# Attention and two feed-forward layers on one core: head pairs of one token block last, first quads in another product order, second token pair's down pass in halves, weight steps reordered

## The chip, the cores and the metric

The kernel runs on one core of a Trainium2 chip. The metric is the device time of one execution in microseconds. The engines are named as the profile names them: PE (TensorE matmuls), PEld (its weight loads), DVE (VectorE), ACT (ScalarE), POOL (GpSimd) and SP (SyncE, here the queue that issues nearly all DMAs; SPq in the trace).

## The reference

```python
# q, k, v: (4, 12, 448, 64); w_in (768, 2048), moe_w_out (2048, 768)
# w_gate, w_val (768, 1536), moe2_w_out (1536, 768); the weights arrive as float64
q_n, k_n = rmsnorm(q, g_q), rmsnorm(k, g_k)
attn = softmax(q_n @ k_n^T / 8)
x = (attn @ v).transpose(0, 2, 1, 3).reshape(1792, 768)
h = np.maximum(x @ w_in, 0.0)
x = h * h @ w_out                               # layer 0
g = x @ w_gate
out = (g * sigmoid(g) * (x @ w_val)) @ w_out2   # layer 1
```

## The kernel before, in words

The 1792 tokens are four token blocks of 448, one for each batch; channels and hidden units lie on the 128 partitions. All arrays between the stages live in one tile, `xacc`, cut into 24 slots of 128x448; slot 6t+c holds channel block c of token block t.

**Attention** runs over 24 head pairs (`pairs`, six for each token block, in the order of the blocks). For each pair the loop issues score matmuls, exponentials, sums and the product with v. The last step of a pair is long: sums are copied out of PSUM, sent to another layout by DMA, added (`total`, L648, POOL), inverted (`recip`, L654, DVE), sent through DRAM and broadcast (`rb<-row`), and only then multiplied in (`xnorm`, L665, POOL); it comes two to three pairs later, and for the last pairs inside the first layer, through a list `drain`.

**Up passes.** x @ w_in (layer 0) and x @ w_gate, x @ w_val (layer 1) are done by a Strassen-Winograd form: for a pair of token blocks (`tp` 0 or 1) and a "quad" of two weight columns blocks (`q_`), seven products P1 to P7 of sums of weight quarters and sums of input quarters. The input operands are B11, B21, B22 and T1 to T4, where T1 to T4 are differences made by `combine` (L124, 128x1344, DVE) in place of the quarter they replace. Each operand is split into a high part (`hi3`, L141, ACT) and a low part (`lo3`, L145, DVE or POOL) in one of 14 "units" (tiles xab, xat, xbb, xbt, xlast). The table `where` says which unit holds which operand. A product (`group`, L881) is 9 matmuls: three channel blocks by high-high, high-low, low-high. PSUM accumulates over products: chain c1 is P1 then P2, c2 is P5 then P3, c3 is P6 then P7 then P4, and `after` (L846 and L849) reads a chain out after each product, so the next product of a chain waits for that read-out. One call of `step` is one product, with the read-out and what the schedule adds to it.

The order of all work on each engine is written out by hand. `plan_types` lists at which step each operand is made. The weight operands come from a generator, `stream`: `convert` turns a float64 slab that a DMA brought (L213) into float32 by four instructions (ACT L243, DVE L244, DVE L224 twice), `block` splits a weight operand into one of five `ring` buffers (ACT L367, DVE L227). `pump(budget)` is called in every step and issues the next stream instructions until the DVE budget is spent or an instruction's gate is closed. The first two quads are interleaved (`paired`), the others follow one by one (`mid`).

**Down passes.** The hidden arrays are written to DRAM (`send`, L842). At the end of an up pass, the stream goes on with the down weights, half rows of 128x384, whose high and low parts go to units that the last quad has freed (`wunits`, gated by `state["down"]`). In the down pass an "item" is 18 matmuls (L1058, 3.65 us of them): for tokens blocks 0 and 1 together it is one hidden block times three output blocks (first half of the outputs, then second half), for blocks 2 and 3, one after the other, one hidden block times six output blocks. `stage` (L998) reads hidden arrays back, four items ahead; `cleave` splits them two items ahead (ACT L1010, DVE L846 at 128x448) into the units `hunits`; the finished outputs are copied out by L1078 and L1080.

## Time and profile before

| | |
|---|---|
| median of 3 runs | 1260.59 us (1260.13 to 1262.28) |
| the profiled execution's own time | 1261.24 us |
| its span | 1259.1 us |
| PE busy | 1194.9 us (95%), 6416 matmuls |
| DVE, ACT, POOL busy | 810.5, 592.0, 376.1 us |
| attention | start to 253.2 us |
| layer 0, up and down | 253.2 to about 743 us |
| layer 1, up and down | about 743 to 1259 us |

Busy is the time in which an engine executed something; a PE that is busy can still run at half its clock, which the column PEclk shows (1.00 is 2.4 GHz, 0.50 is 1.2 GHz). Matmuls are counted in a stretch with those that overlap its borders.

### The profile page before, as it was taken

To read this page: it belongs to the slowest core of one execution; us is meant where nothing else is said; L and a number is where in the kernel's file an instruction comes from. 1 tells how busy PE (TensorE), PEld (TensorE's weight loads), DVE (VectorE), ACT (ScalarE), POOL (GpSimd) and SP (SyncE) were. 2 spreads that over 40 slices of the span, in tenths; PEclk is the share of its full clock that TensorE was granted. 3 is DMA by queue.
4 is the path that set the end of the run, shared out by engine and by line. 5 is a ranking of instruction groups with operands and counts; after the bars stand their busy time and mean duration, and the time that the engine had idled before them with its cause. 6 is when DMAs were issued, how large, how long until landed. Compare 5 with 4: busy or idle time off the path is not lost.

```text
span 1259.1 us, 17643 instructions
## 1 busy us (share of the span) xinstructions
PE 1194.9 (95%) x6416; PEld 1003.0 (80%) x6416; DVE 810.5 (64%) x1177; ACT 592.0 (47%) x1029; POOL 376.1 (30%) x314
## 2 busy tenths in 40 slices
PE   8999999887999995989999999999999996989998
PEld 5556555476999994868999999999999995879997
DVE  7778988776867756776622439767766768773221
ACT  6877886544666545454421344434334343442121
POOL 6889999455001100000010444222312312000000
PEclk9999999998999997999999999999999998999999
DMA  5344341111643436665522202322432326662331
GB/s 157 97 130 122 95 117 46 27 57 34 208 149 116 142 121 218 203 209 181 172 68 66 59 8 98 105 94 66 133 97 89 102 70 210 202 228 83 115 103 59
DMA packets 109190, 146.64 MB, mean 116 GB/s; under 512 B 13104, under 2 KB 101936, under 8 KB 109104
## 3 DMA queue, kind: packets, MB, share of 16 engines
q1 hardware_dynamic: 108784, 145.52, 37.3%
q8 instruction: 50, 0.82, 0.3%
q14 instruction: 36, 0.29, 0.1%
q10 hardware_dynamic: 320, 0.00, 0.0%
HBM read 114.03 MB, written 31.28 MB: 115 GB/s over the span
## 4 chain that ended last, share of the span: by engine, by line
PE 42%; DVE 4%; ACT 2%; issue 1%; DMA 1%; POOL 0%; SPq 0%; ACTq 0%; DVEq 0%
PE ps L881 23%; PE ps L1058 20%; DVE conv L224 2%; DMA xacc<-hid 1%; DVE conv L244 1%; ACT conv L243 0%; POOL xab L145 0%; DVE xab L846 0%; DVE xacc L846 0%; ACT xab L1010 0%; DVE xbt L846 0%; ACT xacc L849 0%; DVE xbt L227 0%; SPq L998 0%; DVE xacc L124 0%
## 5 line engine op out<-in xcount | busy, mean ns | idle before, releaser
L846 POOL TENSOR_TENSOR xacc<-xacc 128x448 f32<-128x448 f32 x76 | 101.1, 1338 | 357.2 <-ACT xacc L849 260.4
L881 PE MATMUL ps<-xat,ring 128*128 128x448 f32 x720 | 160.5, 374 | 15.4 <-DVE xacc L846 8.1
L881 PEld LDWEIGHTS ps<-xat,ring 128*128 128x128 f32 x720 | 139.0, 194 | 27.9 <-issue 8.4
L224 DVE SCALAR_TENSOR_TENSOR conv<-xacc,conv 128x384 int32<-128x384 int32 (+1 forms) x184 | 149.5, 813 | 4.4
L846 DVE TENSOR_TENSOR xacc<-ps,xacc 128x448 f32<-128x448 f32 x188 | 115.4, 619 | 54.4 <-PE ps L881 52.7
L881 PE MATMUL ps<-xbt,ring 128*128 128x448 f32 x540 | 119.8, 370 | 8.7 <-ACT xbt L141 4.6
L227 DVE TENSOR_TENSOR ring<-conv,ring 128x384 fp32r<-128x384 f32 x120 | 83.7, 699 | 65.4 <-ACT ring L367 63.8
L881 PE MATMUL ps<-xbb,ring 128*128 128x448 f32 x540 | 118.5, 369 | 3.0 <-ACT xacc L849 3.0
L881 PE MATMUL ps<-xab,ring 128*128 128x448 f32 x540 | 117.0, 366 | 1.9 <-ACT xacc L849 1.9
L881 PEld LDWEIGHTS ps<-xbt,ring 128*128 128x128 f32 x540 | 102.4, 190 | 18.2 <-ACT xbt L141 5.0
L881 PEld LDWEIGHTS ps<-xbb,ring 128*128 128x128 f32 x540 | 102.6, 190 | 11.7 <-ACT xacc L849 3.4
L881 PEld LDWEIGHTS ps<-xab,ring 128*128 128x128 f32 x540 | 101.3, 188 | 11.1 <-ACT xacc L849 2.3
L367 ACT CAST ring<-conv 128x384 fp32r<-128x384 f32 x120 | 60.9, 510 | 100.9 <-PE ps L881 59.3
L568 DVE TENSOR_REDUCE mxz<-s 112x2 f32<-112x896 f32 x96 | 99.7, 1086 | 11.9 <-PE s L565 11.6
L846 DVE TENSOR_TENSOR xat<-xacc,xat 128x448 fp32r<-128x448 f32 x65 | 44.7, 701 | 93.2 <-ACT xat L1010 93.2
L600 POOL TENSOR_TENSOR sg<-p 112x896 f32<-112x896 f32 x46 | 98.9, 2151 | 16.3 <-ACT p L596 16.3
L849 ACT ACTIVATE xacc<-xacc 128x448 f32<-128x448 f32 x132 | 75.8, 577 | 53.9 <-DVE xacc L846 52.3
L596 ACT ACTIVATE p<-s 112x896 f32<-112x896 f32 x96 | 87.9, 920 | 22.2 <-PE s L594 16.7
L849 ACT ACTIVATE xacc<-ps 128x448 f32<-128x448 f32 x108 | 58.2, 543 | 75.9 <-PE ps L881 66.4
L1010 ACT CAST xat<-xacc 128x448 fp32r<-128x448 f32 x65 | 35.6, 563 | 95.7 <-PE ps L1058 70.4
L846 DVE TENSOR_TENSOR xab<-xacc,xab 128x448 fp32r<-128x448 f32 x48 | 29.3, 623 | 78.6 <-ACT xab L1010 74.3
L244 DVE TENSOR_SCALAR conv<-conv 128x384 int32<-128x384 int32 (+1 forms) x96 | 51.6, 537 | 43.5 <-ACT conv L243 41.5
(128 smaller groups left out, 2121.8 us busy)
## 6 DMA issues: line engine op xcount, KB each, us to landing
xacc<-hid SPq DMA_DIRECT2D x168, 224.0 KB
hid<-xacc SPq DMA_DIRECT2D x112, 224.0 KB
xacc<-in_moe_w_out_dram SPq DMA_DIRECT2D x56, 384.0 KB
xacc<-in_moe_w_in_dram SPq DMA_DIRECT2D x12, 768.0 KB
xacc<-in_moe_w_gate_dram SPq DMA_DIRECT2D x12, 768.0 KB
xacc<-in_moe_w_val_dram SPq DMA_DIRECT2D x12, 768.0 KB
raw<-in_k_dram SPq DMA_DIRECT2D x24, 224.0 KB
raw<-in_q_dram SPq DMA_DIRECT2D x24, 224.0 KB
```

The source lines that it names most:

```text
L224: nc.vector.scalar_tensor_tensor(out=out, in0=in0, scalar=scalar, in1=out, op0=op, op1=ALU.bitwise_or)
L227: nc.vector.tensor_tensor(out=out, in0=a, in1=b, op=ALU.subtract)
L244: yield dve(0.6 * cost, lambda: nc.vector.tensor_scalar(out=ci, in0=ci, scalar1=3, scalar2=0x7FFFFFFF, op0=ALU.logical_shift_left, op1=ALU ...
L367: fn(*args)
L568: nc.vector.tensor_reduce(out=mxz[:, c, 0:P:D], in_=ps[:CP, :, :S], op=ALU.max, axis=AX.X)
L596: nc.scalar.activation(out=p, in_=ps[:CP, :, :S], func=AF.Exp)
L600: nc.gpsimd.tensor_tensor(out=sg, in0=p_t[pi, 2 * w], in1=p_t[pi, 2 * w + 1], op=ALU.add)
L846: eng.tensor_tensor(out=o, in0=a, in1=b, op=op)
L849: nc.scalar.activation(out=slot(s), in_=src, func=func)
L881: nc.tensor.matmul(ps, w[:, wi, kk * P:(kk + 1) * P], xk[:, xi, kk * S:(kk + 1) * S], start=bool(first and mm == 0), stop=(mm == 3 * KT - ...
L1010: nc.scalar.copy(k[:, 0], src)
L1058: nc.tensor.matmul(ps[t, o], w[:, wi, o % KT * P:(o % KT + 1) * P], h[:, hi], start=(f == 0 and n == 0), stop=(f == nf - 1 and n == 2),)
```

## The change

What it does, by parts:

- **Attention.** The last three head pairs of token block 2 are done after those of block 3. The four `combine`s of token pair 0 stand at pairs 15, 17, 19 and 20 (before: 19 to 22); T1 and T3 of token pair 0 are split in the last two iterations. `prep_early` issues two stream instructions for DVE in pairs 3 to 8, then one, and none from pair 21 on (before: one from pair 3 to the end). The first four weight slabs land in `xacc` slots 16 to 23, two buffers, and the single buffer `wraw` is gone.
- **First quads.** The products go P1, P5, P3, P6, P7, P2, P4 (before P1, P2, P5, P6, P3, P7, P4), each for both quads and one token pair, then for both quads and the other. P3 is now copied out by ACT and added to P1 on POOL, P6 is added to that by DVE. The eight PSUM banks are fixed tiles handed out first in, first out. The `drain` and the operand plans are rewritten for the new order.
- **Down pass, layer 0.** Token blocks 2 and 3 are done as a pair, in halves of the outputs, as blocks 0 and 1 are; the operands of layer 1's up pass are made earlier, their low parts on DVE and no longer on POOL. `cleave` is split in a high and a low part, the read-out of a finished half stands ahead of them, and `stage` behind.
- **Down weights.** The stream's order within and between half rows is changed so that the next half's ACT instruction is issued between two DVE instructions of this one. The pump's budget in the last quad is 1.2 a step (before 1.6), in a down item 1.0 and 1.05 (before 2.1).

The diff, cut:

```diff
-    hunits = ((3, 10), (2, 12))
-    wunits = ((0, 7, 4, 11, 1, 8, 2, 9, 5, 12, 6), (13, 5, 7, 6, 10, 11, 0, 1))
+    hunits = ((3, 10), (4, 9))
+    wunits = ((0, 7, 4, 11, 1, 8, 2, 9, 5, 12, 6), (13, 2, 1, 12, 0, 3, 7, 5))
...
-    loose = set()
+    loose = set(range(16, 24))
...
-                at_ = ("nat",) if ph == 0 and n < 2 else (0, 1) if n < 2 or f == 0 else (2, 3)
+                at_ = (0, 1) if (ph and n < 2) or f == 0 else (2, 3)
...
-        paired = [(p, q_) for p in ("P1", "P2", "P5", "P6", "P3", "P7", "P4") for q_ in range(2)]
+        paired = [(p, q_) for p in ("P1", "P5", "P3", "P6", "P7", "P2", "P4") for q_ in range(2)]
...
-            late = None
-            for n in range(2 * NF[ph]):
+            late, n_w = None, 2 * NF[ph]
+
+            def half_ops(n):
+                nonlocal i
                 c = convs[i % NCONV][:, :KH]
+                i += 1
+                return c, convert(i - 1, c, 0.5)
+
+            cur = half_ops(0)
+            yield next(cur[1])
+            for n in range(n_w):
+                c, ops = cur
...
+                ops = list_ops = [op for op in (next(ops, None), next(ops, None)) if op]
+                rest = cur[1]
+                if ops:
+                    yield ops[0]
+                if n + 1 < n_w:
+                    cur = half_ops(n + 1)
+                    yield next(cur[1])
+                if ops:
+                    yield ops[1]
                 if late:
                     yield late
-                yield act(nc.scalar.copy, t[:, 0], c)
+                yield from rest
+                yield act(nc.scalar.copy, t[:, 0], c, gate=lambda n=n, ph=ph: state["down"] >= 100 * ph + n // 6)
                 late = dve(0.55, low_half, ph, n, t, c)
...
-            pairs = [(b, hp) for b in range(B) for hp in range(NPAIR)]
+            pairs = [(b, hp) for b in range(2) for hp in range(NPAIR)] + [(2, hp) for hp in range(KT)]
+            pairs += [(3, hp) for hp in range(NPAIR)] + [(2, hp) for hp in range(KT, NPAIR)]
...
-                elif 19 <= i < 23:
-                    combine(0, ("T1", "T3", "T2", "T4")[i - 19])
-                if i >= 3:
-                    prep_early(1)
+                if i in (15, 17, 19, 20):
+                    combine(0, {15: "T1", 17: "T3", 19: "T2", 20: "T4"}[i])
+                if 3 <= i < 21:
+                    prep_early(1 if i >= 9 else 2)
+                if i == np_ - 1:
+                    lo3(0, 0, "T1")
+                    hi3(0, 0, "T3")
+                    lo3(0, 0, "T3")
...
+                elif i == np_ - 2:
+                    hi3(0, 0, "T1")
...
-            drain.extend([(0, xnorm, np_ - 3), (0, total, np_ - 2), (0, recip, np_ - 2), (2, total, np_ - 1),
-                          (2, recip, np_ - 1), (2, xnorm, np_ - 2), (4, xnorm, np_ - 1)])
+            drain.extend([(1, total, np_ - 2), (1, recip, np_ - 2), (2, xnorm, np_ - 3), (4, total, np_ - 1),
+                          (4, recip, np_ - 1), (6, xnorm, np_ - 2), (9, xnorm, np_ - 1)])
...
+        idle_banks = list(range(8))
 
         def bank():
-            state["turn"] += 1
-            return banks[state["turn"] // 4 % 2].tile([P, 512], F32, tag="ps", name="ps")[:, :S]
+            return idle_banks.pop(0)
...
-            elif p == "P6":
+            elif p == "P6" and not paired:
                 s = L["u2"] = take()
-                tt(nc.vector, slot(s), L["c3"], slot(L["p1"]))
+                tt(nc.vector, slot(s), ps, slot(L["p1"]))
+            elif p == "P3" and paired:
+                s = L["u2"] = take()
+                fun(s, ps, AF.Copy)
+                later(1, tt, nc.gpsimd, slot(s), slot(L["p1"]), slot(s))
...
+            if p in ("P2", "P3", "P4"):
+                idle_banks.append(L[chains[p]])
...
-            todo = [("P1", 0, 0), ("P1", 1, 0), ("P2", 0, 0), ("P2", 1, 0),
-                    ("P1", 0, 1), ("P1", 1, 1), ("P2", 0, 1), ("P2", 1, 1)]
-            todo += [(p, q_, tp) for p, q_ in paired[4:] + mid for tp in range(2)]
+            todo = [(p, q_, tp) for n in range(0, 14, 2) for tp in range(2) for p, q_ in paired[n:n + 2]]
+            todo += [(p, q_, tp) for p, q_ in mid for tp in range(2)]
...
-                step(ph, p, q_, tp, 1.0 if state["down"] < 100 * ph else 1.6)
+                step(ph, p, q_, tp, 1.0 if state["down"] < 100 * ph else 1.2)
...
+        def places(ph, i):
+            nf = NF[ph]
+            if i < 2 * nf:
+                return (3, 4, 5, 9, 10, 11, 12, 13, 14, 15)
+            if ph:
+                return (20, 21, 22, 23)
+            return (12, 13, 14, 15, 20, 21, 22, 23) if i < 3 * nf else (15, 16, 17, 21, 22, 23)
...
-            dn_seq.extend([(t, f)] for t in (2, 3) for f in range(nf))
+            if ph:
+                dn_seq.extend([(t, f)] for t in (2, 3) for f in range(nf))
+            else:
+                dn_seq.extend([(t, f) for t in (2, 3)] for _ in range(2) for f in range(nf))
...
-                if i + 2 < len(dn_seq):
-                    for args in dn_seq[i + 2]:
-                        cleave(ph, *args)
...
-                stage(ph, i + 4)
...
+                ahead_ = dn_seq[i + 2] if i + 2 < len(dn_seq) else ()
+                for args in ahead_:
+                    cleave(ph, *args, 0)
                 for fn in plan.get(i, ()):
                     fn()
-                pump(2.1)
+                pump(1.0)
+                for args in ahead_:
+                    cleave(ph, *args, 1)
+                stage(ph, i + 4)
+                pump(1.05)
...
         plan_types(0, [
...
+            (0, "h", 1, "B11", None), (0, "l", 1, "B11", None), (1, "c", 1, "T1", None), (1, "h", 1, "T1", None),
+            (2, "l", 1, "T1", None), (3, "h", 0, "T2", None), (3, "l", 0, "T2", g), (4, "h", 1, "B22", None),
+            (4, "l", 1, "B22", None), (5, "c", 1, "T3", None), (6, "c", 1, "T2", None), (6, "h", 0, "T4", None),
+            (6, "l", 0, "T4", g), (8, "h", 1, "T2", None), (8, "l", 1, "T2", None), (11, "h", 1, "T3", None),
+            (11, "l", 1, "T3", g), (14, "h", 1, "B21", None), (14, "l", 1, "B21", None), (16, "c", 1, "T4", None),
+            (17, "h", 1, "T4", None), (18, "l", 1, "T4", None),
```

## Rows read from the trace of the kernel before

**Rows 1.** The page: the clock granted to PE, in tenths, in 40 equal slices.
```profile
PEclk9999999998999997999999999999999998999999
```

**Rows 2.** Busy time by stretch: PE, PEld, DVE, ACT, POOL, clock, DMA share, GB/s.
```profile
253.20:320.90 67.70, 54.45 (x244) 48.20 (x241) 46.39 (x48) 33.37 (x50) 35.34 (x17) 0.90 0.22 67
337.30:438.60 101.30, 101.30 (x501) 93.90 (x500) 73.32 (x115) 59.44 (x111) 11.06 (x8) 1.00 0.45 142
458.90:592.70 133.80, 113.39 (x501) 95.96 (x500) 94.72 (x192) 64.60 (x135) 1.15 (x1) 0.94 0.60 188
...
1039.70:1127.90 88.20, 71.07 (x301) 59.91 (x301) 66.67 (x129) 36.85 (x79) 7.04 (x6) 0.90 0.67 210
1150.00:1250.00 100.00, 100.00 (x485) 90.81 (x485) 21.76 (x35) 17.95 (x32) 0.00 (x0) 1.00 0.24 74
```

**Rows 3.** Timeline of PE at the start of layer 0; brackets: idle before, releaser.
```profile
259.04 3.93 PE L881 MATMUL ps<-xab,ring 128*128 128x448 f32 x18 [1.92 <-ACT xacc L849]
...
269.62 5.48 PE L881 MATMUL ps<-xbb,ring 128*128 128x448 f32 x18 [3.00 <-ACT xacc L849]
...
289.00 0.74 PE L881 MATMUL ps<-xbt,ring 128*128 128x448 f32 x1 [4.60 <-ACT xbt L141]
293.47 3.36 PE L881 MATMUL ps<-xbt,ring 128*128 128x448 f32 x8 [3.73 <-DVE xbt L145]
```

**Rows 4.** Timeline of PE at the two ends of an up pass.
```profile
481.32 3.70 PE L881 MATMUL ps<-xat,ring 128*128 128x448 f32 x9 [8.06 <-DVE xacc L846]
...
1054.11 6.38 PE L881 MATMUL ps<-xat,ring 128*128 128x448 f32 x18 [7.32 <-ACT xat L367]
```

**Rows 5.** Timeline of ACT, end of layer 0's up pass.
```profile
478.19 0.52 ACT L243 ACTIVATE conv<-xacc 128x384 f32<-128x384 f32 x1
...
482.18 0.53 ACT L243 ACTIVATE conv<-xacc 128x384 f32<-128x384 f32 x1
```

**Rows 6.** Groups of DVE instructions, 505 to 600 us: count, busy, mean ns.
```profile
L224 DVE SCALAR_TENSOR_TENSOR conv<-xacc,conv 128x384 int32<-128x384 int32 x42 | 23.3, 554 | 0.7
L846 DVE TENSOR_TENSOR xat<-xacc,xat 128x448 fp32r<-128x448 f32 x24 | 14.2, 620 | 10.5 <-ACT xat L1010 10.5
...
L244 DVE TENSOR_SCALAR conv<-conv 128x384 int32<-128x384 int32 x21 | 7.5, 357 | 12.4 <-ACT conv L243 12.4
L227 DVE TENSOR_TENSOR xab<-conv,xab 128x384 fp32r<-128x384 f32 x6 | 3.3, 551 | 0.0
```

**Rows 7.** Busy time by stretch in the down passes, columns as in rows 2.
```profile
510.00:590.00 80.00, 73.05 (x333) 60.99 (x333) 58.94 (x122) 38.87 (x82) 0.00 (x0) 1.00 0.63 202
1080.00:1120.00 40.00, 34.73 (x158) 28.55 (x156) 28.61 (x60) 19.09 (x42) 0.00 (x0) 1.00 0.65 204
627.00:743.00 116.00, 115.90 (x571) 106.89 (x570) 35.99 (x46) 31.55 (x47) 28.50 (x9) 1.00 0.20 54
```

**Rows 8.** Waits of PE, 510 to 595 us and 1080 to 1130 us: us, times, longest.
```profile
PE ps L1058 <- ACT xacc L1080: 2.1, 1, 2.1
...
PE ps L1058 <- ACT xacc L1080: 3.4, 1, 3.4
```

**Rows 9.** Timeline of DVE and PE in pairs 20 to 23 of attention.
```profile
205.52 1.55 DVE L124 TENSOR_TENSOR xacc<-xacc 128x1344 f32<-128x1344 f32 x1
...
215.94 6.75 DVE L124 TENSOR_TENSOR xacc<-xacc 128x1344 f32<-128x1344 f32 x1
...
224.34 0.46 PE L565 MATMUL s<-th 64*112 64x448 f32 x2 [2.34 <-DVE th L552]
...
244.68 0.46 PE L594 MATMUL s<-nm,ones 64*112 64x448 f32 x2 [1.86 <-ACT nm L580]
```

**Rows 10.** Groups of POOL and ACT instructions over the whole span.
```profile
L846 POOL TENSOR_TENSOR xacc<-xacc 128x448 f32<-128x448 f32 x76 | 101.1, 1338 | 357.2 <-ACT xacc L849 260.4 <-DVE xacc L846 84.7 <-ACT ring L367 12.1
L665 POOL TENSOR_TENSOR xacc<-xu,rb 128x448 f32<-128x448 f32 x24 | 29.5, 1228 | 19.1 <-DMA rb<-row 18.6
L145 POOL TENSOR_TENSOR xat<-xacc,xat 128x1344 fp32r<-128x1344 f32 x6 | 21.6, 3596 | 4.7 <-ACT xat L141 4.7
```

More of the change, by code (lines that the diff above doesn't have):

```diff
@@ L69 @@
     clock = {"n": 0}
-    state = {"turn": 1, "used": 0, "debt": 0.0, "down": -1, "limit": 1 << 30}
+    state = {"turn": 1, "used": 0, "debt": 0.0, "down": -1, "limit": 4}
     def slot(s):
@@ L292, in stream @@
                 yield from block((ph, "P1", q_), quads[q_, 0][0])
-            for q_ in range(2):
-                yield from block((ph, "P2", q_), quads[q_, 0][1])
             def first_sum(q_):
@@ L816, in moe, with ps_of @@
             psum[side].close()
-            banks.append(ctx.enter_context(tc.tile_pool(name=f"pp_{side}", bufs=4, space=PSUM, side=side)))
+            pool = ctx.enter_context(tc.tile_pool(name=f"pp_{side}", bufs=1, space=PSUM, side=side))
+            for n in range(4):
+                banks.append(pool.tile([P, 512], F32, tag=f"{side}{n}", name="ps"))
+        idle_banks = list(range(8))
         def bank():
-            state["turn"] += 1
-            return banks[state["turn"] // 4 % 2].tile([P, 512], F32, tag="ps", name="ps")[:, :S]
-        state["turn"] = -1
+            return idle_banks.pop(0)
+        def ps_of(n):
+            return banks[n][:, :S]
         open_units("xbb", (7, 8, 9))
@@ L906, in after @@
                     g = gates.pop((f, t))
[L907 removed]
+                    tt(nc.vector, slot(s), ps, slot(g), ALU.mult)
                     free.append(g)
@@ L930, in step @@
             load_raws()
-            while types and types[0][0] <= clock["n"]:
-                types.pop(0)[1]()
+            run_types()
             after(ph, p, q_, tp)
@@ L967, in up @@
                 if q_ == last and tp == 1 and p == "P7":
-                    for args in dn_seq[0]:
-                        cleave(ph, *args)
+                    for lo in range(2):
+                        for args in dn_seq[0]:
+                            cleave(ph, *args, lo)
             while due:
@@ L973, in up @@
             stage(ph, 3)
-            for args in dn_seq[1]:
-                cleave(ph, *args)
+            for lo in range(2):
+                for args in dn_seq[1]:
+                    cleave(ph, *args, lo)
         dn, hl, dn_seq, dn_list = {}, {}, [], []
@@ L985, in stage @@
                 i, t, f = dn_list[count["s"]]
+                ok_ = places(ph, i)
                 if i < 2 * nf:
-                    s = next((s for s in free if 3 <= s < 6 or 9 <= s < 16), None)
-                    if s is None:
-                        return
-                    free.remove(s)
-                    held[t, f] = s
-                else:
-                    if i == 2 * nf:
-                        assert not any(set(a) & {2, 3} for n, (_, a) in enumerate(loads) if n in sent and n not in turned)
-                        loose.difference_update(range(20, 24))
-                    s = 20 + i % 4
+                    s = next((s for s in free if s in ok_), None)
+                else:
+                    s = next((s for s in ok_ if s not in held.values()), None)
+                if s is None:
+                    return
+                if i < 2 * nf:
+                    free.remove(s)
+                elif s >= 16:
+                    assert not any(n in sent and n not in turned and set(a) & {s // 20 * 2, s // 20 * 2 + 1}
+                                   for n, (_, a) in enumerate(loads))
+                    loose.discard(s)
+                held[t, f] = s
                 dn[t, f] = slot(s)
@@ L1048, in down @@
                 f = items[0][1]
-                half = i // nf if i < 2 * nf else None
+                half = None if len(items) == 1 else i // nf % 2
                 os = range(KD) if half is None else range(half * KT, (half + 1) * KT)
```

148 lines of the change are left out of this document (65 added, 83 removed), and 3 rows, old and new, of the table fn.

## The prediction

> **What bounds the kernel now.** I read the clock slices first, then busy time by stretch, then PE's timeline where a stretch loses time, then the engine that PE waits for there. The clock is full except in slices around three places: the start of layer 0 and the two ends of an up pass [rows 1]. Where nothing disturbs PE, 500 matmuls take 101.30 us, so 0.2026 us each [rows 2]; this is the yardstick. It makes a product of 9 matmuls 1.82 us and a down item of 18 matmuls 3.65 us. By it four stretches lose time [rows 2], if the weight loads are taken as the count:
>
> - start of layer 0, 253.20 to 320.90: 67.70 - 241 x 0.2026 = 18.9 us
> - end of layer 0's up pass and first half of its down pass, 458.90 to 592.70: 133.80 - 500 x 0.2026 = 32.5 us
> - the same place of layer 1, 1039.70 to 1127.90: 88.20 - 301 x 0.2026 = 27.2 us
> - the last 127 us: 100 us hold 485 matmuls, 0.2062 each, a loss of 1.7 us in 100, 2.2 us in all.
>
> That is 80.8 us in which PE has work and is late with it. Everything else behind attention runs at the yardstick, so PE is the bound, and a change can win no more than these 80.8 us there, and little in attention, where PE waits 2.34 and 1.86 us near its end [rows 9].
>
> Why each is lost. **Start of layer 0:** PE waits 1.92 and 3.00 us for ACT's copy of P1 before P2 may go on in the same chain, and 4.60 and 3.73 us for T2 of token pair 1 (ACT's high part, DVE's low part) [rows 3], which hangs on the last head pairs, those of block 3. The rest is PE at half clock behind these waits. **Ends of the up passes:** P4 of the last quad follows P7 in chain c3 and waits for DVE's read-out (8.06 us), and in layer 1 for ACT's ring cast (7.32 us) [rows 4]. DVE isn't too slow there, it is in lock step with ACT: a half row of down weights starts every 3.99 us (478.19, 482.18) [rows 5], while its DVE instructions take 0.357 + 2 x 0.554 + 0.551 = 2.02 us [rows 6]. Each engine waits for the other in turn, and read-outs stand in the same queues. **First half of the down passes:** in 80 us 333 matmuls, 12.5 us lost, in 40 us 158, 8.0 us lost [rows 7]. DVE is busy 74% and 72% of these [rows 7], so this too is lock step, plus 2.1 and 3.4 us for PSUM read-outs by ACT [rows 8].
>
> **The change, part by part.**
>
> *New product order and pair order.* P2 comes 20 products behind P1, so its wait for the copy goes; each chain now has at least three other products between two of its own. B11, B22, T1, T2 and T3 of token pair 1 no longer need the last three head pairs; only B21 (products 23 and 24) and T4 (27 and 28) do, over 20 products, 36 us, after the start. The waits of rows 3 go, and the half clock with them. What is late next: B11 of pair 1 is wanted by the third product; bounded by nothing and the 1.92 us of the wait that stands there now, I take 0.3. Then POOL: 8 adds for P5 and P3 (1.338 each), three low parts (3.596 each) and four `xnorm` (1.228 each) [rows 10] are 26.4 us of work to be done by the nineteenth product, which begins at 33 us, and some of it waits for ACT and for the broadcasts. DVE's P6 read-out stands behind the POOL add of P3, and P7 behind that read-out: I take 2 us there and 1.7 us for the rest, 4 in all. Bounds: 0 and the 18.9 of now. Gain **14.9**. The 8 read-outs that go from DVE to ACT and POOL in both layers cost nothing else; in layer 1 only one low part goes to POOL in that time, 8 x 1.338 + 3.596 = 14.3 us in the same 33.
>
> *Down weights and pump.* With the next half row's ACT instruction issued between two of DVE's, and the low part of the previous half row between the last two, DVE always has an instruction whose ACT partner is done. Then a half row costs its DVE time, 2.02 us, not 3.99. In the last quad the pump gives 1.2 a step, a half row costs 1.85 of it, so 0.65 x 2.02 = 1.31 us, and 0.62 for a read-out by the same shape [rows 6]: 1.93 us against 1.82. Over the ten products in which half rows are made DVE falls 1.1 us behind; before it was 0.86 x 3.99 = 3.45 us a step without the read-out. Fewer half rows are ready when the down pass begins (6.5 by the budget, 8.6 before), which costs nothing as long as one is made for each item. The new gate asks for the arrival of half row n+1 inside n, which with four buffers allows three in three items, just one each. In the down pass DVE then has 2.02 + 2 x 0.62 = 3.26 us an item of 3.65. The read-outs of a finished half now stand ahead of `cleave`, so 2.1 and 3.4 us go [rows 8]. I leave for each layer 1 us at P4, 3 at the first two items (the casts behind the last read-outs) and 4 in the rest: 8. Bounds: 3 (the first items alone) and 16 (half of 32.5). Gains 32.5 - 8 = **24.5** and 27.2 - 8 = **19.2**.
>
> *Second token pair in halves, layer 0.* 32 more reads, casts and subtractions, nine low parts from POOL to DVE, one more `combine`. In 627 to 743 us DVE is busy 36.0 of 116 us [rows 7]; with 32 x 0.62 + 10 x 1.55 [rows 9] it is 71.3. ACT's 31.6 become some 51 by the same 0.62. Read traffic goes from 54 by 32 x 0.229 MB / 116 us = 63 to 117 GB/s, against 188 and 210 that the queue moves elsewhere [rows 2]. SP issues the reads behind the low parts that free their slots, two items (7.3 us) ahead of the cast. PE's 116 us of matmuls hide this; if a low part, a combine, two subtractions and the pump meet in one item (1.55 + 1.55 + 1.24 + 2.2 = 6.5 us), the two items of lead cover it. The wait that it removes is small, for layer 1's start is at the yardstick already. Cost **1.4**, bounds 0 and 6 (four such meetings, 1.5 each).
>
> *Attention.* The waits of 2.34 and 1.86 us [rows 9] come from a `combine` that took 6.75 us and from a ring cast queued ahead of the negated maximum. The second goes with `prep_early`, which stops at pair 21. Four combines now stand in pairs 15, 17, 19 and 20: one took 1.55 us without a wait of PE, one 6.75 with 2.34 [rows 9]; halfway, 4 x 1.17 = 4.7 against 4.2 now: cost **0.5**, bounds -4.2 and +5.2. One more stream instruction in each of pairs 3 to 8 is hidden by PE's matmuls as the one of now is; without that cover it costs its own time, some 2 x 0.554 for twice the width [rows 6], 6 x 1.1 = 6.6 us, which I add to the upper bound alone.
> The Trainium skill, page SBUF — State Buffer, section Who interferes with whom, says that a VectorE instruction with two SBUF inputs and a GpSimd one that reads SBUF exclude each other, and that whoever comes second waits. It speaks against two more combines among POOL's normalisations: by it each may cost the 2.34, 4 x 2.34 = 9.4, and the sum would be 4.7 us higher. The 6.75 us beside 1.55 for one shape agrees, the 1.55 says that it need not happen.
>
> *Last stretch.* 0.2062 or 0.2026: what decides isn't in the trace; half of 2.2, gain **1.1**. Renamed units, the slab buffers in `xacc` (the same four loads) and fixed banks issue nothing; their cover is the same waits as now.
>
> Sum: 14.9 + 24.5 + 19.2 + 1.1 - 1.4 - 0.5 = 57.8. From the profiled execution's own 1261.24 that leaves 1203.4; the median of the runs is 0.65 lower, so 1202.8, **1203 us**.
>
> **Rivals.**
>
> *DMA takes over in the first half of the down passes.* An item there needs a half row (0.393 MB) and two hidden arrays (0.459 MB); at the 202 to 204 GB/s that it moves now [rows 7] that is 4.18 us, not 3.65: 0.53 x 56 items = 29.7, and 4 at each start, 37.7 where I left 16. **1224 us.** For it: one queue, in order. Against: the reads wait now for slots and buffers that the lock step frees late, so the 203 is no limit that was tried. Chance 0.12.
>
> *Lock step remains.* ACT's casts could still queue behind copies that wait for PE. Then only the two waits of rows 4 go, 15.4, by the lower budget: 14.9 + 15.4 - 1.9 = 28.4. **1232 us.** Against: the partner instruction now lies one DVE instruction ahead. 0.12.
>
> *Nearly everything goes.* All of the 80.8 and 4.2 us but 5: **1181 us.** Against: the first two items need casts behind the last read-outs. 0.09.
>
> *Slower: the second half of layer 0's down pass becomes bound by the loop read, cast, subtract, free slot.* Six slots for three items of 3.65 us; it decides where that loop makes an item longer than 3.65 + 57.8/32 = 5.5 us; at 6 us an item the 32 cost 32 x 2.35 = 75 us, 1202.8 + 75 = **1278 us**. Against: DVE at 61% there. 0.05.
>
> *The change does nothing that counts,* other waits ending at the same times: 1260 us. 0.02.
>
> **How the numbers follow.** My own case has 0.60 and, with 4 us either way at the start of layer 0 and 5 at each up end and in attention, reaches from 1190 to 1216. The range 1184 to 1230 takes in the DMA case and half of the best one and leaves out the lock step, slower and idle cases, some 0.2. About 0.2% is what a measurement of this kernel can tell from no change. Faster by over 0.2%: all but the last two, 0.93; same 0.02; slower 0.05.
>
> **What would show it.** Right: full clock at all three places, no wait of PE over 2 us at P2, P4 or T2, half rows about 2 us apart, some 490 matmuls in 100 us in the first half of both down passes. Wrong: a P7 of the first quads waiting over 5 us for POOL's adds; casts of hidden arrays waiting for DMA; DVE near 100% after 620 us with PE below its yardstick; pairs 15 to 20 longer than their neighbours by several us.

## The result, and the profile after

Measured: **1221.84 us** (median of 4 runs, 1216.92 to 1226.56) beside 1260.36 for the kernel before in the same session; the ratio is 0.9693, 95% interval 0.9647 to 0.974. The forecast was 1203, range 1184 to 1230. The change is faster, by two thirds of what was forecast: 38.5 us of 57.8. The profiled execution took 1226.56 us, the slowest of the four; what follows is read from it.

The clock slices of the changed kernel's page; beside [rows 1] the dips at the start of layer 0 and at the two ends of the up passes are gone, and one in attention (184 to 214 us) is new:

```profile
PEclk9999998999999999999999999999999999999999
```

Busy time by stretch of the changed kernel, columns as in [rows 2]. The cuts stand at the same matmuls as in the kernel before: attention, start of layer 0 (240 matmuls), rest of its up pass (680), end and first half of its down pass (500), second half (740), layer 1's up pass (1460), its end and first half of down (300), the rest.

```profile
2.00:266.90 264.90, 249.95 (x1881) 144.91 (x1881) 204.97 (x236) 187.28 (x289) 208.46 (x206) 0.98 0.34 94
266.90:323.50 56.60, 50.58 (x242) 46.13 (x241) 41.71 (x36) 32.54 (x53) 26.69 (x16) 0.97 0.24 80
323.50:463.90 140.40, 140.40 (x681) 127.59 (x681) 97.92 (x154) 81.51 (x154) 15.21 (x11) 1.00 0.45 144
463.90:569.00 105.10, 102.66 (x502) 93.60 (x502) 86.97 (x185) 64.67 (x132) 1.15 (x1) 1.00 0.77 245
569.00:727.30 158.30, 154.07 (x741) 139.72 (x740) 90.86 (x133) 63.76 (x106) 0.00 (x0) 0.99 0.41 126
727.30:1029.10 301.80, 301.80 (x1462) 274.07 (x1462) 210.06 (x294) 119.76 (x212) 83.10 (x59) 1.00 0.28 90
1029.10:1096.00 66.90, 62.24 (x302) 55.99 (x301) 56.31 (x112) 34.34 (x71) 9.25 (x6) 1.00 0.83 269
1096.00:1220.60 124.60, 124.60 (x616) 115.47 (x615) 37.61 (x67) 29.48 (x56) 0.00 (x0) 1.00 0.32 100
```

Between the same matmuls the kernel before took 251.2, 67.7, 138.0, 133.8, 150.5, 296.5, 88.2 and 127.1 us. So by stretch, against the terms of the sum (us; a plus is longer):

| stretch | measured | forecast | missed by |
|---|---|---|---|
| attention | +13.7 | +0.5 | 13.2 |
| start of layer 0 | -11.1 | -14.9 | 3.8 |
| up passes, undisturbed part | +2.4, +5.3 | 0 | 7.7 |
| layer 0, end and first half down | -28.7 | -24.5 | -4.2 |
| layer 0, second half down | +7.8 | +1.4 | 6.4 |
| layer 1, end and first half down | -21.3 | -19.2 | -2.1 |
| last stretch | -2.5 | -1.1 | -1.4 |

The misses add up to 23.4; the profiled execution lies 23.2 above the 1203.4 of the sum, the median 19.0 above 1202.8. The two ends won 50.0 us, more than the whole net gain of 34.4 in these stretches; four stretches got longer.

Waits of PE at the ends of the up passes (464 to 500 us, then 1029 to 1096; us, times, longest), where [rows 4] had 8.06 and 7.32:

```profile
PE ps L899 <- DVE xacc L864: 0.9, 1, 0.9
...
PE ps L1100 <- ACT xat L1056: 1.4, 1, 1.4
...
PE ps L899 <- DVE xacc L864: 1.9, 2, 1.2
PE ps L1100 <- ACT xat L1056: 1.7, 1, 1.7
```

ACT's timeline there: two half rows start 2.20 us apart, 3.99 in [rows 5], and two of the first in the down pass 2.75:

```profile
477.82 0.54 ACT L238 ACTIVATE conv<-xacc 128x384 f32<-128x384 f32 x1
...
480.02 0.54 ACT L238 ACTIVATE conv<-xacc 128x384 f32<-128x384 f32 x1
...
495.38 0.56 ACT L238 ACTIVATE conv<-xacc 128x384 f32<-128x384 f32 x1
...
498.13 0.56 ACT L238 ACTIVATE conv<-xacc 128x384 f32<-128x384 f32 x1
```

The 2.20 is not a steady pace: the half rows just behind it start 5.61, 4.20, 1.75 and 3.81 us apart. The down pass shows the pace: 2.75 us for a few of them, then mostly 3.65, one for each item, where the kernel before mostly needed 3.99.

PE's timeline in the places that lost time or kept some (in attention, at layer 0's start, in the second half of its down pass):

```profile
184.62 0.71 PE L570 MATMUL s<-th 64*112 64x448 f32 x2 [3.94 <-DVE th L557]
...
288.06 1.89 PE L899 MATMUL ps<-xbb,ring 128*128 128x448 f32 x8 [2.50 <-DVE xbb L145]
293.48 3.45 PE L899 MATMUL ps<-xbb,ring 128*128 128x448 f32 x9 [3.52 <-ACT xacc L867]
...
607.25 5.54 PE L1100 MATMUL ps<-xat,xab 128*128 128x448 f32 x26 [1.00 <-DVE xat L864]
620.98 6.97 PE L1100 MATMUL ps<-xat,xbb 128*128 128x448 f32 x26 [2.52 <-DVE xat L864]
634.42 5.64 PE L1100 MATMUL ps<-xat 128*128 128x448 f32 x26 [0.70 <-DVE xat L864]
```

### The profile page after: what moved, and what is told of

Same layout as the page of the kernel before. It is cut to its first block, busy times and chain, and to the rows that moved or that the text cites. A ratio compares the mean times of both kernels' runs of the same rounds, so it can differ in the third digit from the quotient of the medians.

```text
span 1224.8 us, 17794 instructions
## 1 busy us (share of the span) xinstructions
PE 1186.7 (97%) x6416; PEld 997.5 (81%) x6416; DVE 827.9 (68%) x1215; ACT 614.9 (50%) x1069; POOL 344.8 (28%) x308
## 4 chain that ended last, share of the span: by engine, by line
PE 82%; DVE 6%; DMA 4%; issue 4%; ACT 3%; POOL 1%; SPq 0%; DVEq 0%; ACTq 0%; POOLq 0%
PE ps L899 38%; PE ps L1100 30%; PE s L599 5%; PE s L614 4%; PE s L570 2%; DMA hid<-xacc 2%; PE s L635 1%; PE s L538 1%; DMA xacc<-hid 1%; DVE conv L219 1%; DVE xacc L864 1%; DVE mxz L573 1%; DVE xacc L124 1%; POOL qk L520 1%; ACT xacc L867 1%
## 5 line engine op out<-in xcount | busy, mean ns | idle before, releaser
L864 POOL TENSOR_TENSOR xacc<-xacc 128x448 f32<-128x448 f32 x84 | 117.3, 1405 | 637.4 <-ACT xacc L867 547.9
L219 DVE SCALAR_TENSOR_TENSOR conv<-xacc,conv 128x384 int32<-128x384 int32 (+1 forms) x192 | 157.6, 821 | 2.8
L864 DVE TENSOR_TENSOR xacc<-ps,xacc 128x448 f32<-128x448 f32 x180 | 110.5, 620 | 60.3 <-PE ps L899 50.0
L899 PEld LDWEIGHTS ps<-xat,ring 128*128 128x128 f32 x720 | 135.0, 188 | 14.6 <-ACT xbb L372 1.2
L864 DVE TENSOR_TENSOR xat<-xacc,xat 128x448 fp32r<-128x448 f32 x113 | 68.3, 627 | 82.8 <-ACT xat L1056 82.8
L222 DVE TENSOR_TENSOR ring<-conv,ring 128x384 fp32r<-128x384 f32 x116 | 74.6, 644 | 67.0 <-ACT ring L372 66.5
L1056 ACT CAST xat<-xacc 128x448 fp32r<-128x448 f32 x113 | 62.7, 567 | 110.1 <-PE ps L1100 88.5
L605 POOL TENSOR_TENSOR sg<-p 112x896 f32<-112x896 f32 x46 | 104.9, 2280 | 21.5 <-ACT p L601 21.5
L899 PEld LDWEIGHTS ps<-xbt,ring 128*128 128x128 f32 x540 | 101.3, 188 | 11.1 <-DVE xacc L864 1.1
L899 PEld LDWEIGHTS ps<-xab,ring 128*128 128x128 f32 x540 | 101.3, 188 | 10.7 <-issue 0.7
L867 ACT ACTIVATE xacc<-ps 128x448 f32<-128x448 f32 x116 | 62.3, 545 | 76.7 <-PE ps L899 71.1
L1100 PE MATMUL ps<-xat,xab 128*128 128x448 f32 x405 | 87.6, 367 | 3.4 <-DVE xat L864 2.1
L599 PE MATMUL s<-th 64*112 64x448 f32 x576 | 80.0, 383 | 5.5 <-ACT xu L623 3.7
```

The lines of the kernel that those rows point to most:

```text
L219: nc.vector.scalar_tensor_tensor(out=out, in0=in0, scalar=scalar, in1=out, op0=op, op1=ALU.bitwise_or)
L222: nc.vector.tensor_tensor(out=out, in0=a, in1=b, op=ALU.subtract)
L599: nc.tensor.matmul(ps[:CP, a, :S], lhs, rhs, start=(w == 0), stop=(w == 3))
L605: nc.gpsimd.tensor_tensor(out=sg, in0=p_t[pi, 2 * w], in1=p_t[pi, 2 * w + 1], op=ALU.add)
L864: eng.tensor_tensor(out=o, in0=a, in1=b, op=op)
L867: nc.scalar.activation(out=slot(s), in_=src, func=func)
```

## The experiments

Eleven kernels, in the order of the question. The stretch of the profile decides where a total can't, since the runs of one kernel differ by up to some 10 us, for a reason argued in the last section. Of each kernel one execution has a profile.

### Was it the lock step? The half rows alone, both ways

First the changed kernel with the old order of a half row's instructions. With the order the gate moves too, from the last instruction of a half row back to its first:

```diff
...
-                if ops:
-                    yield ops[0]
-                if n + 1 < n_w:
-                    cur = half_ops(n + 1)
-                    yield next(cur[1])
-                if ops:
-                    yield ops[1]
+                ops = convert(i, c, 0.5)
+                i += 1
+                op = next(ops)
+                yield op[:4] + (lambda g=op[4], n=n, ph=ph: g() and state["down"] >= 100 * ph + n // 6,)
+                for k, op in enumerate(ops):
+                    yield op
+                    if k == 1 and late:
+                        yield late
+                        late = None
                 if late:
                     yield late
-                yield from rest
-                yield act(nc.scalar.copy, t[:, 0], c, gate=lambda n=n, ph=ph: state["down"] >= 100 * ph + n // 6)
+                yield act(nc.scalar.copy, t[:, 0], c)
```

> The changed kernel with only the order of the down-weight instructions as it was before (each half row's ACT instruction behind the previous half row's last DVE instruction, gate on its first instruction); the pump's budgets stay as changed. Theory A, the lock step of ACT and DVE is what cost time at the ends of the up passes and in the first half of the down passes: the stretch of 500 matmuls at layer 0's end rises from 105 to 122 to 134 us, that of 300 at layer 1's end from 67 to 78 to 88 us, the whole by 28 to 50 us, and half rows are again 3.4 to 4 us apart. Rival B, the lower budget or the order of cleave and read-outs did it: the two stretches grow by less than 10 us together.

1252.71 us, ratio 0.9934 [0.9906, 0.9962]. Its two ends by stretch, and two of ACT's half rows, now 3.44 us apart (in the first half of its down pass 2.92 to 4.97):

```profile
461.60:588.10 126.50, 108.99 (x501) 94.76 (x501) 90.06 (x185) 62.25 (x131) 1.15 (x1) 0.97 0.63 203
...
1037.20:1120.00 82.80, 67.20 (x303) 58.47 (x302) 61.10 (x120) 35.06 (x75) 7.82 (x6) 0.94 0.68 217
```
```profile
476.69 0.54 ACT L238 ACTIVATE conv<-xacc 128x384 f32<-128x384 f32 x1
480.13 0.54 ACT L238 ACTIVATE conv<-xacc 128x384 f32<-128x384 f32 x1
```

The ends lose 21.4 + 15.9 = 37.3 us of the 50.0, as theory A had it, and PE waits 6.1 us for one read-out by DVE again. Then the reverse, the kernel before with the new order of a half row alone, gate included:

> The kernel before with one part of the change alone: the new order of a half row's instructions, with its gate. Theory A (the lock step was the loss at the two ends, and this order alone lifts it): the two stretches at the ends of the up passes fall from 133.8 and 88.2 us to about 107 and 69, the start of layer 0 stays near 67.7 and attention near 251; 1213 to 1228 us, about where the whole change stands, which would mean that all its other parts add up to little. Theory B (the gain needs the read-outs ahead of the casts and the fixed banks as well): both stretches keep most of their length, 120 and 80 or more, 1240 us or more.

**1212.6 us**, ratio 0.9617 [0.9564, 0.967]. By stretch (start of layer 0, the two ends, and between them the second half of layer 0's down pass):

```profile
255.90:322.40 66.50, 56.01 (x245) 49.61 (x242) 45.66 (x47) 32.92 (x49) 33.80 (x15) 0.87 0.22 69
460.50:567.00 106.50, 103.96 (x502) 93.62 (x501) 87.40 (x183) 63.97 (x132) 1.16 (x1) 1.00 0.74 235
567.00:719.90 152.90, 152.90 (x742) 138.85 (x741) 63.97 (x87) 46.76 (x74) 28.80 (x9) 1.00 0.28 86
...
1016.40:1085.60 69.20, 64.24 (x301) 57.41 (x301) 59.05 (x114) 34.15 (x70) 7.93 (x6) 0.98 0.83 262
```

Theory A holds: 27.3 + 19.0 = 46.3 of the 50.0 us come from one reordering and its gate, which weren't tried apart; the change's other parts add 3.7 at the ends to that, and 12.7 without it. The run also shows what the rest of the change does: its interval meets that of the whole change only at the edge, and its median is 9 us lower. Without the new order of products and pairs the start of layer 0 keeps 66.5 us, so that part is worth 9.9; attention (253.9 here, 264.9 there) and the second half of the down pass (152.9, 158.3) cost 16.4.

### Where attention lost 13.7 us

DVE's timeline in pair 15 of the changed kernel, and PE's stretch from 184 us on. Two instructions that prepare later pairs (L475, L116) come first, then a combine and a stream instruction, each slower than its plain time (1.55 in [rows 9], 0.55 for the stream's); PE waits 3.94 us and then runs at a granted clock of 0.53:

```profile
174.36 1.21 DVE L475 TENSOR_REDUCE ss<-sq 112x16 f32<-112x1024 f32 x1
175.48 0.98 DVE L116 TENSOR_TENSOR xab<-xacc,xab 128x448 fp32r<-128x448 f32 x1
176.39 3.52 DVE L124 TENSOR_TENSOR xacc<-xacc 128x1344 f32<-128x1344 f32 x1
179.83 3.61 DVE L222 TENSOR_TENSOR conv<-conv,conv 128x384 f32<-128x384 f32 x1
```
```profile
184.00:191.00 7.00, 6.38 (x38) 4.63 (x38) 5.65 (x7) 2.17 (x3) 3.08 (x2) 0.53 0.10 34
```

So: no stream instruction in a pair that holds a combine.

```diff
-                if 3 <= i < 21:
+                if 3 <= i < 21 and i not in (15, 17, 19, 20):
```

> The changed kernel in which pairs 15, 17, 19 and 20, those with a combine, issue no stream instruction ahead of time. Theory A, it is the combine together with a second contended DVE instruction (3.52 and 3.61 us in pair 15) that makes PE wait: the step from pair 15 to 16 falls from 16.5 to 10 to 12 us, the four steps behind a combine together lose at most 5 us over 9.65 each (now 11.4), and attention ends 5 to 8 us earlier. Rival B, the combine alone does it: the four steps still lose over 9 us. Rival C, the stream instructions that now come later delay the start of layer 0 by as much as is won.

1215.89 us, 0.9639 [0.9601, 0.9677]; the stretch falls by 8.0 us, and the step from pair 15 to 16 (from the first product with V of one pair to that of the next) from 16.48 to 10.40:

```profile
2.00:258.90 256.90, 246.23 (x1881) 142.63 (x1881) 204.70 (x232) 187.14 (x288) 208.82 (x206) 0.99 0.34 97
```

The combines still took 3.52 twice: the time of one alone fits under PE's matmuls, that of two doesn't. Of theory C there is 1.4 us, 58.0 at the start of layer 0 in place of 56.6.

The second loss is early: ACT's square waits for a load of q that was requested behind two weight slabs of 768 KB, in the queue that brings both, from ACT's timeline of the changed kernel:

```profile
37.63 1.06 ACT L468 ACTIVATE sq<-raw 112x1024 f32<-112x1024 f32 x1 [2.58 <-DMA raw<-in_q_dram]
```

```diff
-                load_raws()
+                if i >= 4:
+                    load_raws()
...
-                    prep_early(1 if i >= 9 else 2)
+                    prep_early(1 if i >= 11 else 2)
```

> The changed kernel with the first two weight slabs requested from pair 4 on, not from pair 0, and the pairs with two stream instructions moved to 3 to 10. Theory A, the two slabs of 768 KB stand in the one DMA queue ahead of q and k of pair 4 and ACT waits 2.58 us for them: the step from pair 1 to 2 falls from 13.74 to about 9.7 us and no other step grows by as much; attention ends about 4 us earlier. Rival B, the slabs cost the same wherever they stand (they delay another pair's load): the 4 us come back at a later step.

1215.46 us, 0.9641 [0.9616, 0.9666]; the stretch falls by 7.2 us, and the step from pair 1 to 2 goes from 13.74 to 9.69 us, without that wait:

```profile
2.00:259.70 257.70, 247.72 (x1881) 144.36 (x1881) 203.96 (x234) 187.41 (x289) 206.89 (x206) 0.99 0.34 97
```

How far these sizes can be trusted is shown by four other experiments that leave attention as the change has it (the old half rows above; below, the subtractions first, the low parts and the additions on VectorE). Attention took 261.9 to 263.4 us in them, the step from pair 1 to 2 10.6 to 11.9 (ACT waited 1.0 to 2.3 us for q in each), and the long step stood behind pair 17, 14.6 to 17.9 us. So the profiled execution of the change is on the long side, and against these four the edits win less, 5.0 to 6.5 us and 4.2 to 5.7; the long step and the wait for q are there every time.

Both edits together:

> Changed kernel with both attention edits together: no preparation instruction in the four pairs that hold a combine, and the first weight slabs requested from pair 4 on. Theory A (two independent losses, each shown alone): attention falls from 264.8 us by the sum of the two, 8.0 + 7.1, to 249 to 252, near the 251.2 of the kernel before; the whole 1204 to 1211 us. Theory B (preparation that is pushed later meets the last pairs or the start of layer 0): attention 254 or more, or the start of layer 0 60 or more, the whole 1213 or more.

**1207.54 us**, 0.9579 [0.9552, 0.9606], with attention at 250.8, start of layer 0 at 59.6, and layer 1's up pass:

```profile
2.00:252.80 250.80, 244.37 (x1881) 142.01 (x1881) 199.62 (x230) 186.95 (x288) 206.26 (x206) 1.00 0.36 100
252.80:312.40 59.60, 53.13 (x245) 47.45 (x242) 45.05 (x45) 33.94 (x55) 31.08 (x16) 0.94 0.25 80
714.90:1010.80 295.90, 295.90 (x1462) 274.19 (x1461) 209.55 (x293) 119.17 (x212) 83.56 (x59) 1.00 0.29 92
```

Theory A: 14.1 of 8.0 + 7.2 = 15.2 us, and the whole of the attention term is explained. 3.0 of it are given back at the start of layer 0, where more of the stream's instructions now stand on VectorE (45 instructions there in place of 36).

### The second half of layer 0's down pass

In the changed kernel ACT waits 6.08 us for a read of a hidden half, DVE 4.98 for ACT's conversion queued behind that cast, and only then come the conversion and the subtraction that PE wants at 620.98. ACT's and DVE's timelines:

```profile
611.08 1.13 ACT L1056 CAST xbt<-xacc 128x448 fp32r<-128x448 f32 x2 [6.08 <-DMA xacc<-hid]
```
```profile
617.84 0.56 DVE L239 TENSOR_SCALAR conv<-conv 128x768 int32<-128x768 int32 x1 [4.98 <-ACT conv L238]
618.44 1.95 DVE L219 SCALAR_TENSOR_TENSOR conv<-xacc,conv 128x768 int32<-128x768 int32 x2
620.31 1.15 DVE L864 TENSOR_TENSOR xat<-xacc,xat 128x448 fp32r<-128x448 f32 x2
```

```diff
+                early_ = ph == 0 and i >= 2 * nf
+                if early_:
+                    for args in ahead_:
+                        cleave(ph, *args, 1)
+                    stage(ph, i + 4)
                 for fn in plan.get(i, ()):
                     fn()
                 pump(1.0)
...
```

> Changed kernel, but in the second half of layer 0's down pass the subtractions of the hidden halves and the next reads are issued ahead of the pumped conversion and of the types. Theory A (the loop read, cast, subtract, free slot stalls there because slab conversions stand ahead of the subtractions that free the slots): PE's waits of 1.00, 2.52 and 0.70 us go, the stretch falls from 158.3 us to 150 to 153, the whole by 5 to 8. Theory B (the reads are late because 768 KB slabs stand between them in the one queue): the waits stay, the stretch stays at 156 or more. The rhythm of PE moves the whole by some 6 us either way, so the stretch decides and not the total.

1217.69 us, 0.9667 [0.9634, 0.9699]; the stretch falls only to 154.9, above A's 153 and below B's 156, and some 1.6 of these 3.4 us are the faster of PE's two rhythms (last section; an estimate, 400 matmuls at 0.2024 and not 0.2064 us). In its trace one conversion (602.40 us) still stood ahead of the subtractions at the turn into that half, and one slab request (605.89) ahead of the next reads. Next, with the attention edits in, the edit begins two items earlier and the slab requests go behind the reads:

```diff
-                load_raws()
+                if ph or i < 2 * nf - 2:
+                    load_raws()
...
+                early_ = ph == 0 and i >= 2 * nf - 2
...
                     stage(ph, i + 4)
+                    load_raws()
```

> The changed kernel with both attention edits, and from two items before the second half of layer 0's down pass on the subtractions of the hidden halves and the next reads stand ahead of types and pump, with the slab requests behind those reads. Theory A (the rest of the stall there, 4.7 us with the subtractions first from the next item on, was one conversion ahead of the subtractions at the turn and a slab ahead of a read): the stretch falls from 156.9 us to 150 to 153, the whole to 1201 to 1205. Theory B (four slots are too few: a read waits for its slot whatever the order): the stretch stays at 154 or more, the whole at 1205 to 1208.

1202.55 us, 0.9543 [0.9512, 0.9575]. The stretch took 156.9 us with the attention edits alone; now it is 153.1, and PE's waits for ACT and DVE from 540 to 720 us are 0.5, 0.3 and 0.2:

```profile
557.10:710.20 153.10, 152.09 (x742) 138.73 (x741) 90.81 (x133) 63.85 (x106) 0.00 (x0) 1.00 0.41 129
```

The slots suffice (theory B falls); who stands ahead of the subtraction, and of the read, decides. Which of the two moves did it, the earlier start or the slab behind the reads, wasn't tried apart. The changed kernel with the old half rows says the same from another side: its reads are the same, and that half took 153.2 us with 2.0 us of waits, so it isn't the halves as such that cost.

### What stays at the start of layer 0

In the changed kernel B22's low part, plain time 1.55, took 9.07 us beside GpSimd's additions and low parts (DVE's timeline):

```profile
278.94 9.07 DVE L145 TENSOR_TENSOR xbb<-xacc,xbb 128x1344 fp32r<-128x1344 f32 x1
```

First the three low parts of GpSimd moved to VectorE (three rows of `plan_types(0, ...)`: `g` to `None`):

> The changed kernel with the three low parts that its first operand plan still gives to POOL (T2 and T4 of token pair 0, T3 of pair 1) on DVE. Theory A, DVE and POOL exclude each other on instructions that read two SBUF operands: the low part of B22 that took 9.07 us on DVE takes some 1.6, PE's waits of 2.50 and 3.52 us in the first 57 us of layer 0 go, and that stretch (240 matmuls, 56.7 us in the changed kernel, 48.6 at the yardstick) comes to 50 to 51 us. Rival B, DVE simply has too much to do there: three more low parts of 1.56 us each make the stretch 57 to 61 us. The rest is unchanged, so the whole moves by about -6 us by A and 0 to +4 by B, besides what the matmul rhythm (0.2027 or 0.2067 us) does to long stretches.

1222.91 us, 0.9691 [0.964, 0.9742]; the start takes 55.9 us. The 9 us instruction is gone, its neighbours pay (2.52 for a low part, 1.50 for a ring subtraction), and P7 waits for P6's read-out behind them, 2.35 and 2.46 us. So neither theory holds as put, A's 50 to 51 or B's 57 to 61. PE's timeline:

```profile
296.98 2.09 PE L899 MATMUL ps<-xat,ring 128*128 128x448 f32 x9 [2.35 <-DVE xacc L864]
301.53 3.35 PE L899 MATMUL ps<-xat,ring 128*128 128x448 f32 x9 [2.46 <-DVE xacc L864]
```

Then the eight additions instead:

```diff
             elif p == "P5":
                 s = L["p5"] = take()
-                fun(s, ps, AF.Copy)
-                later(1, tt, nc.gpsimd, slot(s), slot(L["p1"]), slot(s))
+                if paired and ph == 0:
+                    tt(nc.vector, slot(s), ps, slot(L["p1"]))
+                else:
...
```

> Changed kernel, but the P5 and P3 read-outs of the first quads of layer 0 are single VectorE additions out of PSUM (8 of 0.62 us) in place of a ScalarE copy and a GpSimd addition. Theory A (what remains of the loss at the start of layer 0 comes from VectorE and GpSimd instructions that hold each other up, the additions among them): the start falls from 56.7 us to 50 to 53, and the low part of B22 no longer takes 9 us. Theory B (VectorE is simply too full there, 8 more instructions of 0.62 us make it later still): 57 to 60. Theory C (the three low parts on GpSimd are enough to hold VectorE up): 55 to 57, the 9 us instruction stays.

1221.17 us, 0.9703 [0.966, 0.9746]; 55.8 us, with one wait of 5.11 in place of two. No theory fits whole: the length is C's, but the 9 us instruction is gone as A had it. So both moves at once, on the kernel of 1202.55, whose start took 58.5:

> The kernel of the run above, with the three low parts and the eight additions of layer 0's start all on VectorE, so that GpSimd has only the normalisation of the last heads there. Theory A (the instructions of the two engines hold each other up, so either move alone only passed it on): the start falls from 59.6 us to 51 to 54, and no VectorE instruction of 128x1344 takes over 2 us after the last head. Theory B (VectorE is full there, so the work that comes to it, 3 x 1.55 + 8 x 0.62 = 9.6 us, is late in its turn): 58 or more, with waits for VectorE's read-outs and low parts while these take their plain time.

1203.45 us, 0.9544 [0.9518, 0.9569]. The start of layer 0 as a whole and 10 us of it, and PE's timeline:

```profile
252.20:310.00 57.80, 52.34 (x245) 47.49 (x242) 43.05 (x54) 30.43 (x47) 5.99 (x5) 0.91 0.24 81
270.00:280.00 10.00, 7.45 (x21) 6.25 (x22) 10.00 (x12) 3.57 (x5) 1.72 (x1) 0.53 0.08 25
```
```profile
271.34 3.70 PE L900 MATMUL ps<-xab,ring 128*128 128x448 f32 x9 [4.25 <-DVE xacc L865]
276.25 3.48 PE L900 MATMUL ps<-xab,ring 128*128 128x448 f32 x9 [1.21 <-DVE xacc L865]
```

My own theory A falls: with GpSimd nearly idle (5.99 us) the start is 57.8 us where it was 58.5, just under B's 58, and VectorE is busy 10.00 of 10 us. P3 waits for the read-outs of P5, its forerunner in chain c2, and these stand in the middle of VectorE's block of work, the next two behind T4's low part. DVE's timeline, the first read-out and that low part:

```profile
270.57 0.62 DVE L865 TENSOR_TENSOR xacc<-ps,xacc 128x448 f32<-128x448 f32 x1
...
273.04 2.53 DVE L145 TENSOR_TENSOR xat<-xacc,xat 128x1344 fp32r<-128x1344 f32 x1
```

If so, an instruction taken out ahead of a read-out gives its time back. The two rows of T4 of token pair 0 go from product 6 to 13:

```diff
-            ... (6, "c", 1, "T2", None), (6, "h", 0, "T4", None),
-            (6, "l", 0, "T4", None), (8, "h", 1, "T2", None), ...
+            ... (6, "c", 1, "T2", None), (8, "h", 1, "T2", None), ...
+            (11, "l", 1, "T3", None), (13, "h", 0, "T4", None), (13, "l", 0, "T4", None),
```

> The kernel of the run above, with the high and low part of T4 of token pair 0 made seven products later at the start of layer 0 (behind product 13; it is used by product 25). Theory A (VectorE works through a block of some 20 us without a gap there, and the read-outs of P3 stand in the middle of it; each instruction taken out of the block ahead of them gives its time back): the low part took 2.53 us and stands behind the first of the two read-outs waited for, so of the waits of 4.25 and 1.21 us the second goes, and of the half clock behind it some: the start falls from 57.7 us to 53 to 56.5, the whole to about 1200. Theory B (the part only moves the burst to the products behind 13, where another read-out waits): 57 or more, with a new wait for VectorE between 282 and 300 us.

(The read-outs meant there are those of P5 that P3 waits for.) **1198.81 us**, 0.9507 [0.9472, 0.9541], the lowest median here, 23 us below the changed kernel's; from 1202.55 and 1203.45 its total can't be told apart. The second wait is gone and the first stays, as theory A had it. The 1.7 us won at the start are little more than the 1.1 by which two kernels with the same start differ (59.6 with the attention edits alone, 58.5 with the next edit); the wait that is gone is the firmer sign. The start, then PE's wait:

```profile
253.40:309.50 56.10, 51.87 (x245) 46.85 (x242) 41.73 (x53) 30.03 (x46) 6.00 (x5) 0.94 0.24 77
```
```profile
272.46 6.10 PE L900 MATMUL ps<-xab,ring 128*128 128x448 f32 x18 [4.24 <-DVE xacc L865]
```

## Why the prediction was right, and where not

**The lock step, right and shown.** The order of the half rows with its gate, alone, wins 46.3 of 50.0 us, and half rows 3.99 us apart became one for each item. The price of 2.02 us a half row was not reached as a pace: 2.20 is one pair, 2.75 the least that holds for several in a row. I left 8 us at each end; by the yardstick of 0.2026 3.8 and 5.9 are left (105.1 - 500 x 0.2026, 66.9 - 301 x 0.2026).

**The DMA rival, wrong.** The queue moved 245 and 269 GB/s in the two stretches, against 188 and 210 in [rows 2] and the 203 that the rival took for a limit. The lock step rival falls by the same stretches, which won 50.0 us and not 15.4.

**Attention, the step that failed.** The forecast had four combines at half the old harm, +0.5; measured was +13.7 (10.7 to 12.2 in the four other kernels with this attention). I took the price of a combine from two rows [rows 9] of the last pairs. A stream instruction stood behind each of them too, at its plain time, DVE's timeline of the kernel before:

```profile
206.99 0.55 DVE L227 TENSOR_TENSOR ring<-conv,ring 128x384 fp32r<-128x384 f32 x1
...
222.62 0.55 DVE L227 TENSOR_TENSOR ring<-conv,ring 128x384 fp32r<-128x384 f32 x1
```

What I missed is where the combines went. No instruction that prepares a later pair stands right ahead of those two; pair 15 has L475 and L116 there, and both the combine and the stream instruction were stretched. Taking the stream instruction out gives 8.0 us back; moving the combines back to the last pairs instead wasn't tried. The other 7.2 I did not price at all: of the additional stream instructions I counted VectorE's time (in the upper bound), not the slabs that they call for, which go into the same queue ahead of q and k. With both, the term went past its upper bound of +11.8 in this profile. The Trainium skill, page SBUF — State Buffer, section Who interferes with whom, has the rule that a VectorE instruction with two SBUF inputs and a GpSimd one that reads SBUF exclude each other; the 3.52 and 3.61 us agree with it. The price that I derived from it, 4.7 us more, was nearer than the one I took.

**Second half of layer 0's down pass: the mechanism seen, its place in the sum too small.** I allowed 1.4, upper bound 6; it cost 7.8, of which 4.2 are waits and most of the rest the half clock and the slower rhythm behind them (last section). I said that two items of lead cover a meeting of instructions. They don't where the read's own start hangs on the subtraction that the meeting delays: that is the loop of the slower rival, at one place instead of 32 items. With the order changed the stretch took 154.9, then 153.1 us.

**Start of layer 0: 11.1 of 14.9.** The waits of [rows 3] went, as forecast. What was late next was B22's low part, and P3 behind the read-out of P5, not P7 as I had it; 7.8 us stay by the yardstick (56.6 - 241 x 0.2026), not 4. I named GpSimd as what is late; the runs say that VectorE's queue fills there whether GpSimd has work or not (57.8 and 58.5 us).

**Up passes, 7.7 us that no step had.** The undisturbed stretches have no waits, and yet took 2.4 and 5.3 us more. I had met this in the last stretch, 0.2062 against 0.2026 a matmul [rows 2], and had written that what decides isn't in the trace, but put it into the sum only there.

That the time fell into the range is due to its width: of the misses 31.1 us went against the forecast and 7.7 for it. Three of the four signs of being wrong that the prediction names came up: casts of hidden arrays waited for DMA (6.08 us), DVE was busy 5.93 of the 6 us from 618 to 624 while PE was busy 3.48, and the step behind pair 15 was 6.8 us longer than the 9.65 of its neighbours.

## What to carry to other kernels

When two engines hand one item back and forth, put the next item's first instruction between the steps of this one: that single reordering, with its gate, was worth more than all the rest of this change. Price an added instruction by what stands behind it in its queue and by the DMA that it calls for earlier, not by its own duration. Where moving work from one engine to another changes nothing, look for the stretch in which the receiving engine is busy 10 of 10 us, and move an instruction in time instead.

## What was not expected of the hardware

At full granted clock PE has two rhythms. Layer 1's up pass, the same 1462 matmuls with no wait, took 301.80 us in the changed kernel (0.2064 each) and 295.90 with the attention edits (0.2024 each). In the profiles here a stretch without a stall keeps one rhythm nearly from its start to its end, and the next may have the other: the last stretch took 127.1 us in the kernel before and 124.6 in the changed one. The profiles of the change and of two experiments (low parts on VectorE, no stream instruction beside a combine) have the slow one in layer 1's up pass, the other ten the fast one; layer 0's undisturbed part took 137.8 in both of these experiments. The two up passes and the last stretch alone can move a run by 11 us (140.4 - 137.8, 301.8 - 295.9, 127.1 - 124.6: 11.0 in sum), about the spread of the changed kernel's four runs (9.6). That the rhythm makes this spread is argued: only one run of a kernel has a profile. What picks the rhythm at a restart stays open; no run here tells.

How far one instruction is stretched beside GpSimd: a VectorE subtraction of 128x1344 took 1.55 us undisturbed, 2.5 and 9.07 beside GpSimd's instructions; a combine, of the same shape, 1.55, 3.52 and 6.75. And taking GpSimd away nevertheless gained next to nothing where VectorE was full.
